# Retention, then a gated two-layer network, on one core: the first 64 positions loaded by pairs of heads in 2 KB runs

## The chip, the core and the metric

The kernel runs on one core of one Trainium2 chip. TensorE (PE) multiplies, VectorE (DVE), ScalarE (ACT) and GpSimd (POOL) work on tiles, SyncE (SP) and also ACT and POOL issue DMA transfers between HBM and the on-chip memories; TensorE writes to PSUM alone, and DVE and ACT bring its results from there to SBUF ("evict" below). The metric is the device time of one execution in microseconds (us), the median of several runs. A profile of one execution is shown beside it; times inside it count from the start of its span.

## What is computed

q, k and v are [8 batches, 8 heads, 576 positions, 64] in float32. Each head computes a decayed causal product, and the heads' outputs, side by side, go as 4608 tokens of 512 through a network with a hard swish:

```python
scores = scale * np.matmul(q, k.transpose(0, 1, 3, 2))
gamma = 1.0 - 2.0 ** (-5.0 - np.arange(H, dtype=np.float32))
Dmat = np.where(rel >= 0, gamma[:, None, None] ** rel[None, :, :], 0.0)
ret = scores * Dmat[None, :, :, :]
attn = np.matmul(ret, v)
x = attn.transpose(0, 2, 1, 3).reshape(B * S, H * D)
h = x @ w_in
g = h * np.clip(h + 3.0, 0.0, 6.0) / 6.0
out = g @ w_out
```

rel is the query's position less the key's; w_in is [512, 2048] and w_out [2048, 512].

## The kernel before

The tokens are worked in nine blocks of 512 (kb). Block 0 holds the first 64 positions (TL) of all eight batches; each later block is the other 512 positions of one batch, in four chunks of 128 with a running state per head. A block goes through the up projection (up_steps and up_pair: 16 units, each eight matmuls ph = win times xT for one 128-wide slice of d_ff, then u on ACT and the gated g on DVE) and the down projection (pd, or pm in a form with fewer products). TensorE's program interleaves the down projection of one block, the up projection of the next and the chunks of later ones. The order of all work is written out by hand: an engine runs its instructions in the order of the calls at the end of the kernel (L768 to L887), and a call that needs something late holds up what stands behind it on that engine.

The change lies in block 0, the head of the kernel. Its 64 x 8 = 512 tokens are four column groups c (NCB = 4) of 128: two batches, c and c + 4, of 64 positions each, since products of two batches are masked away. Its steps:

- load_half (L407) brings q and k in float32, one head for all batches at a time, with four positions (NJ = 4) of 64 numbers, 1 KB, side by side on a partition; a pair of neighbouring heads 2i and 2i + 1 fills a tile. The first k goes over SP and ACT, q over SP and ACT, the other keys over POOL, which also casts them to float16. The q of pairs 2 and 3 and the k of pairs 2 and 3 wait until the first half of k0 has landed (`behind`, `keys`).
- load_values (L422) brings v with one transfer from POOL into raw_v, the win pieces and then the wout pieces follow on the same queue. Loads of chunks 4 and up wait for the third wout piece (fetch, L838).
- indices and distances (L90, L113) make on POOL and DVE the position tables, a permutation by_chunk and the distances; mask_of_heads (L123) makes the decay masks of a pair on ACT.
- cast_heads (L435) casts q and the first k on DVE; turn_heads (L440) turns a tile with matmuls against by_chunk into PSUM (hpt, two banks, tag "st") and evicts it on ACT as kT or qT.
- scores_heads (L471) multiplies kT and qT (hpa) and masks the result on DVE (a16).
- values_heads (L463) orders the values of a pair with 16 matmuls (by_key, hpv) and evicts them on ACT into vh; inner_heads (L485) multiplies vh and a16 (hpo) and copies the result to xT of block 0.
- then the first four units of the up projection start, with the last inner product inside them (L823 to L831).
- during the up projection POOL and ACT make the decay tables (decays, L128) and POOL scales the keys, still by position on the partitions (others, L138); after it keys_heads (L466) orders them with 16 matmuls a pair (hpk) between the first products of the down projection, and head_states (L290) builds the states that the later blocks start from.

idle_products are matmuls whose result is not used; they keep TensorE active while it waits. PSUM has six banks of tag "pp" for hpa, hpv, hpo, hpk, ph and the idle products.

Of the kernel before, what the change touches and what calls it, by code (L numbers as in the profile page):

```python
# [21 lines left out]
def kernel(  # L22
# [13 lines left out]
    P = 128  # L36
# [30 lines left out]
    RP = TL // NJ  # L67
    ii = const.tile([P, NJ + 1], I32)
    ij = const.tile([P, NJ + 6], I32)
    fj = const.tile([P, NJ + 6], FP32)  # L70
    key, odd = fj[:, NJ + 3:NJ + 4], fj[:, NJ + 5:NJ + 6]
    arg = const.tile([P, NJ + 3, 2 * H], FP32)
    dec = const.tile([P, NJ + 3, 2 * H], FP32)
# [7 lines left out]
    dist, far = early[:, 0:P], early[:, P:2 * P]  # L81
    scale = const.tile([P, 1], FP32)
    FAR = 1.0e6
    by_chunk = const.tile([P, P], FP16)
    only = const.tile([P, 2], FP32)
    last = const.tile([P, 1], FP32)
    gpow = const.tile([P, NP], FP32)
    zh = [const.tile([P, NP, D], FP32, name=f"zh{b}") for b in range(B)]

    def indices():  # L90
        nc.vector.memset(half, 0.5)
        nc.gpsimd.iota(ii[:, 0:NJ], pattern=[[0, NJ]], base=0, channel_multiplier=1)
        nc.gpsimd.iota(ii[:, NJ:NJ + 1], pattern=[[1, 1]], base=0, channel_multiplier=1)
        nc.gpsimd.iota(query, pattern=[[TL, 2], [1, NJ], [NJ, RP]], base=0, channel_multiplier=0,
                       allow_small_or_imprecise_dtypes=True)
        make_identity(nc, ident16)
        p_ = ii[:, NJ:NJ + 1]
        nc.vector.tensor_scalar(ij[:, 0:NJ], ii[:, 0:NJ], P - B, 1, ALU.bitwise_and, ALU.logical_shift_right)
        nc.vector.tensor_copy(ij[:, NJ:NJ + 1], p_)
        for e in range(2):  # L100
            nc.vector.tensor_scalar(ij[:, NJ + 1 + e:NJ + 2 + e], p_, SUB - 1, 1, ALU.bitwise_and,
                                    ALU.logical_shift_left)
        nc.vector.tensor_scalar(ij[:, NJ + 3:NJ + 4], p_, RP - 1, 2, ALU.bitwise_and, ALU.logical_shift_left)
        nc.vector.tensor_scalar(ij[:, NJ + 4:NJ + 5], p_, 5, None, ALU.logical_shift_right)
        nc.vector.tensor_scalar(ij[:, NJ + 5:NJ + 6], p_, 4, 1, ALU.logical_shift_right, ALU.bitwise_and)
        nc.vector.tensor_copy(fj, ij)
        nc.vector.tensor_tensor(fj[:, 0:NJ], fj[:, 0:NJ], query[:, 0:TL:RP], ALU.add)
        nc.vector.tensor_scalar(fj[:, NJ:NJ + 2], fj[:, NJ:NJ + 2], 1.0, -float(P // 2), ALU.mult, ALU.add)
        nc.vector.tensor_scalar(fj[:, NJ + 2:NJ + 3], fj[:, NJ + 2:NJ + 3], 1.0, 1.0 - float(P // 2), ALU.mult, ALU.add)
        nc.vector.tensor_copy(by_chunk.rearrange("p (c e r) -> p c e r", c=NCB, e=2),  # L110
                              ident16.rearrange("p (r e c) -> p c e r", e=2, c=NCB))

    def distances():  # L113
        nc.vector.memset(scale, float(np.log(D ** -0.5)))
        nc.vector.tensor_tensor(key, key, fj[:, NJ + 4:NJ + 5], ALU.add)
# [5 lines left out]
        nc.vector.scalar_tensor_tensor(out=dist, in0=query, scalar=key, in1=far, op0=ALU.subtract, op1=ALU.add)  # L121

    def mask_of_heads(i):  # L123

        for h in (2 * i, 2 * i + 1):
            nc.scalar.activation(hmask[:, h, :], dist, ACTF.Exp, bias=scale, scale=float(np.log(gamma[h])))

    def decays():  # L128
        for h in range(H):
            lg = float(np.log(gamma[h]))  # L130
            nc.gpsimd.tensor_scalar(arg[:, :, h], fj[:, 0:NJ + 3], lg, float(np.log(D ** -0.5)),
                                    ALU.mult, ALU.add)
            nc.gpsimd.tensor_scalar(arg[:, :, H + h], fj[:, 0:NJ + 3], -lg, 0.0, ALU.mult, ALU.add)
# [784 lines left out]
```

## Time and profile before

| | us |
|---|---|
| median of 3 runs | 299.74 |
| lowest and highest | 299.30, 299.77 |
| the profiled execution | 299.44 |
| its span, first to last instruction | 297.7 |
| PE busy | 286.3 (96%) |
| DVE busy | 211.3 (71%) |
| ACT busy | 193.8 (65%) |
| POOL busy | 133.4 (45%) |

The mean granted clock of TensorE over the span is 0.994 of the full one. A row of the chain or of the timeline gives the start, the duration, the engine, the line of the kernel, the operation, what it writes and reads, and in brackets the idle time before it with what ended it. A row of the groups gives busy time, the mean of one instruction in ns, and the idle time before them. "PEld" is TensorE's loading of the stationary operand.

### The profile page before, as it was taken

Reading aid. Unit: us, or ns where it says so; the run is one execution under the profiler, and the core shown is the slowest. Engines: PE = TensorE matmul, PEld = TensorE weight load, DVE = VectorE, ACT = ScalarE, POOL = GpSimd, SP = SyncE. Lnnn points to the kernel's source line nnn. Section 1 sums busy time; section 2 is a strip of 40 time slices with the busy share of each in tenths; the row PEclk is TensorE's granted clock in tenths of the full one; section 3 lists DMA queues with packets and bytes.
Section 4 is the critical chain, followed back from the end, with each engine's and each line's share of the span. In section 5 each row is a group of like instructions: output and inputs, shape, how many; then the busy total and the mean of one; then the engine's idle time right before and its main releaser. Section 6 shows DMA issues by size and latency. Waiting matters only on the chain.

```text
span 297.7 us, 12581 instructions
## 1 busy us (share of the span) xinstructions
PE 286.3 (96%) x5552; PEld 218.8 (73%) x5552; DVE 211.3 (71%) x374; ACT 193.8 (65%) x350; POOL 133.4 (45%) x169
## 2 busy tenths in 40 slices
PE   5699999999999999999999999999999999999995
PEld 2467566788556667878988787787787788778894
DVE  5629636669885688798866887787769676647654
ACT  5659875789776687586758577566856665655420
POOL 7665078417851912539614862386256013100510
PEclk9979999999999999999999999999999999999999
DMA  7999998989999999998999999789907101200114
GB/s 163 188 205 216 217 233 206 213 184 221 135 214 221 203 205 196 167 234 191 228 244 194 184 216 174 144 168 263 144 27 118 74 2 39 104 5 2 73 73 141
DMA packets 119430, 47.86 MB, mean 161 GB/s; under 512 B 92240, under 2 KB 114768, under 8 KB 119376
## 3 DMA queue, kind: packets, MB, share of 16 engines
q1 hardware_dynamic: 114336, 41.56, 70.6%
q0 software_dynamic: 4608, 5.11, 10.4%
q8 instruction: 43, 0.70, 1.0%
q10 hardware_dynamic: 432, 0.39, 0.5%
q14 instruction: 11, 0.09, 0.2%
HBM read 36.70 MB, written 9.44 MB: 155 GB/s over the span
## 4 chain that ended last, share of the span: by engine, by line
PE 87%; DVE 4%; DMA 4%; ACT 3%; issue 1%; POOL 1%; ACTq 0%
PE ph L168 41%; PE pm L168 29%; PE pd L168 7%; PE po L250 4%; DMA raw_v<-in_v_dram 3%; PE pa L250 2%; DVE ws L552 2%; PE pu L250 1%; DMA hk<-in_k_dram 1%; ACT u L515 1%; DVE g L516 1%; DVE a L285 1%; POOL hk L416 1%; PE hpo L491 1%; PE hpv L459 1%
## 5 line engine op out<-in xcount | busy, mean ns | idle before, releaser
L168 PE MATMUL ph<-xT,win 128*64 128x512 f16 (+1 forms) x1248 | 144.9, 365 | 0.5 <-DVE g L516 0.3
L537 DVE SCALAR_TENSOR_TENSOR g<-u,ph 128x512 f16<-128x512 f32 x132 | 89.2, 683 | 48.5 <-ACT u L535 47.7
L535 ACT ACTIVATE u<-ph,half 128x512 f32<-128x512 f32 x132 | 90.2, 693 | 43.1 <-PE ph L168 40.6
L168 PEld LDWEIGHTS <-win 128*64 128x64 f16 x1248 | 84.5, 136 | 26.5 <-issue 1.9
L168 PEld LDWEIGHTS <-g 128*64 128x64 f16 x928 | 51.0, 110 | 15.6 <-issue 1.1
L168 PEld LDWEIGHTS <-s 128*64 128x64 f16 x896 | 49.9, 110 | 8.4 <-issue 0.5
L334 POOL TENSOR_TENSOR z<-z,gpow 128x256 f32<-128x256 f32 x24 | 16.4, 685 | 75.3 <-DVE z L333 46.9
L168 PE MATMUL pm<-ws,s 128*64 128x256 f16 x672 | 45.6, 273 | 0.1
L386 ACT CAST xT<-po 128x256 f16<-128x256 f32 (+1 forms) x44 | 22.5, 584 | 23.4 <-PE po L250 23.4
L211 POOL TENSOR_TENSOR q<-fq,dec 128x512 f16<-128x512 f32 x32 | 36.7, 1169 | 0.0
L214 POOL TENSOR_TENSOR v<-fv,dec 128x512 f16<-128x512 f32 x32 | 35.5, 1113 | 1.9 <-DMA fv<-in_v_dram 1.9
L168 PE MATMUL pd<-wout,g 128*64 128x512 f16 x256 | 35.0, 382 | 0.2 <-ACT o L581 0.2
L616 POOL TENSOR_TENSOR u<-u,p 128x512 f32<-128x512 f32 x7 | 8.9, 1271 | 54.0 <-ACT u L656 47.8
L168 PE MATMUL pm<-wout,g 128*64 128x256 f16 x448 | 31.6, 273 | 0.4 <-issue 0.4
L285 DVE TENSOR_TENSOR a<-pa,mask 128x256 f16<-128x256 f32 (+1 forms) x44 | 21.9, 539 | 7.8 <-PE pa L250 7.4
L203 ACT CAST k<-fk 128x512 f16<-128x512 f32 x32 | 19.8, 620 | 0.0
L552 DVE TENSOR_TENSOR s<-g 128x1024 f16<-128x1024 f16 x28 | 19.6, 702 | 0.2
L340 ACT CAST z<-z 128x512 f16<-128x512 f32 x24 | 15.0, 625 | 4.2 <-DVE z L330 3.9
L168 PE MATMUL pm<-ws,g 128*64 128x256 f16 x224 | 16.3, 273 | 0.0
L168 PE MATMUL pm<-wout,s 128*64 128x256 f16 x224 | 16.0, 273 | 0.1
L250 PE MATMUL po<-qT,z 64*64 64x64 f16 x512 | 12.6, 198 | 0.7 <-issue 0.4
L552 DVE TENSOR_TENSOR s<-g,s 128x1024 f16<-128x1024 f16 x14 | 12.6, 903 | 0.0
(112 smaller groups left out, 277.7 us busy)
## 6 DMA issues: line engine op xcount, KB each, us to landing
fq<-in_q_dram SPq DMA_DIRECT2D x16, 512.0 KB, 5.9
fk<-in_k_dram SPq DMA_DIRECT2D x32, 256.0 KB, 4.6
fv<-in_v_dram SPq DMA_DIRECT2D x32, 256.0 KB, 5.7
out_dram<-o SPq DMA_DIRECT2D x14, 512.0 KB, 3.2
wout<-in_moe_w_out_dram POOLq DMA_DIRECT2D x4, 512.0 KB, 18.5
out_dram<-o SPq DMA_DIRECT2D x7, 256.0 KB, 3.9
win<-in_moe_w_in_dram POOLq DMA_DIRECT2D x3, 512.0 KB, 13.4
hq<-in_q_dram SPq DMA_DIRECT2D x6, 128.0 KB, 5.0
```

Of the source, the lines that this page charges most:

```text
L168: nc.tensor.matmul(out[r], lhs[:, r], rhs, skip_group_check=True, **flags)
L203: keys = lambda: nc.scalar.copy(by_head(k16), in_rows(st[c]["fk"]))
L211: nc.gpsimd.tensor_tensor(by_head(q16[:, e]), in_rows(st[c]["fq"][:, :, e, :]), in_rows(dd[:, NJ + 1 + e, 0:H, :]), ALU.mult)
L214: nc.gpsimd.tensor_tensor(v16, st[c]["fv"], dd[:, NJ, H:2 * H, :], ALU.mult)
L250: return lambda: nc.tensor.matmul(*args, skip_group_check=True, **flags)
L285: nc.vector.tensor_tensor(a16[:, a, 0:n].rearrange("p x i q -> p (x i) q"), pa[a].rearrange("p x i q -> p (x i) q"), m, ALU.mult)
L334: nc.gpsimd.tensor_tensor(new, new, decay, ALU.mult)
L340: nc.scalar.copy(z16, zs[c])
L386: nc.scalar.copy(xt[:, s], po[s].rearrange("p x n (e r) -> p x n e r", e=2))
L535: nc.scalar.activation(uu, ph, ACTF.Relu, bias=half, scale=1.0 / 6.0)
L537: nc.vector.scalar_tensor_tensor(out=g[:, hf, :, jr, :], in0=by_half(uu), scalar=1.0, in1=by_half(ph), op0=ALU.min, op1=ALU.mult)
L552: nc.vector.tensor_tensor(*pend.popleft())
```

## The change

The pairs of heads become i and i + 4 (as in the rest of the kernel) in place of 2i and 2i + 1. A tile of q or k is loaded whole by one transfer, with eight positions (JL = 8) of a head, 2 KB, on a partition; the partition is (batch, which of the two heads, group of eight positions). No load waits for another. Turning a tile takes 16 matmuls against sel (64 columns for each of the two heads) in place of 8 against by_chunk; q is written back to the order of positions by the eviction, so the queries are in order and inner_heads copies straight.

The values are ordered by four heads at a time (g) and two column groups (y), eight matmuls of 256 columns each, and are evicted by ACT and DVE in turn, after all four scores. The inner products of column groups 0 and 2 of x come first, those of 1 and 3 follow inside the first units, whose order of the four slices becomes 0, 2, 1, 3; the two halves of the first win piece are slices 0 and 2, then 1 and 3. The fillers are 5, 2, 1, 1, 2 and a short 2 in place of 5, 4, 1, 1 and a short 5.

The keys for the states are now kT: POOL scales it by grown (four exponentials on ACT of a position table), and keys_heads turns it back with 8 matmuls against the identity in place of 16 with by_chunk. distances is folded into indices, which makes sel as well. The diff, cut to its core:

```diff
 def indices():
...
+        for e in range(2):
+            nc.vector.tensor_copy(sel[:, e], ident16.rearrange("p (y c e r) -> p e c y r", y=2, c=NCB, e=2)[:, e])
+        nc.vector.tensor_copy(by_chunk.rearrange("p (c y r) -> p c y r", c=NCB, r=RL),
+                              ident16.rearrange("p (r y c) -> p c y r", r=RL, c=NCB))
...
     def decays():
+        nc.gpsimd.iota(place, pattern=[[1, NJ], [NJ, 2], [0, 2], [JL, RL]], base=0, channel_multiplier=0,
+                       allow_small_or_imprecise_dtypes=True)
...
         nc.scalar.activation(dec, arg, ACTF.Exp)
+        for i in range(NP):
+            nc.scalar.activation(grown[:, i], place, ACTF.Exp, scale=rate[:, i:i + 1])
...
     def others():
         for i in range(NP):
-            k16 = hd[i]["k"].rearrange("p e j d -> p j e d")
-            dd = dec[:, 0:NJ, H + 2 * i:H + 2 * i + 2].unsqueeze(3).to_broadcast([P, NJ, 2, D])
-            nc.gpsimd.tensor_tensor(k16, k16, dd, ALU.mult)
+            kT = hd[i]["kT"]
+            nc.gpsimd.tensor_tensor(kT, kT, grown[:, i].unsqueeze(1).to_broadcast([P, NCB, P]), ALU.mult)
...
-    def load_half(i, nm, e, queue, behind=None):
...
+    def load_heads(i, nm, queue, behind=None):
...
+        d = queue.dma_start(t, dict(q=q, k=k)[nm][:, i::NP, 0:TL, :].rearrange("b e (r j) d -> (b e) r (j d)", j=JL))
...
     def turn_heads(i, nm, copy):
-        pt = psum.tile([P, NJ, P], FP32, tag="st", bufs=2, name=f"hpt{nm}{i}")
-        for j in range(NJ):
+        pt = psum.tile([P, JL, NCB, 2 * RL], FP32, tag="st", bufs=2, name=f"hpt{nm}{i}")
+        for j in range(JL):
+            at = j if nm == "q" else 2 * (j % NJ) + j // NJ
             for e in range(2):
-                nc.tensor.matmul(pt[e * D:e * D + D, j, :], hd[i][nm][:, e, j, :], by_chunk, start=True, stop=True,
+                nc.tensor.matmul(pt[e * D:e * D + D, at], hd[i][nm][:, j * D:j * D + D],
+                                 sel[:, e].rearrange("p c y r -> p c (y r)"), start=True, stop=True,
                                  skip_group_check=True)
...
+        if nm == "q":
+            t = half_tile(work, "qT", i, FP16, "hqT", bufs=3)
+            copy(t.rearrange("p (x j) -> p x j", j=JL), pt.rearrange("p j c y -> p (c y) j"))
+        else:
+            t = work.tile([P, H * D], FP16, tag="kT", bufs=4, name=f"hkT{i}")
+            copy(t.rearrange("p (c j y) -> p c j y", c=NCB, j=JL), pt.rearrange("p j c y -> p c j y"))
...
+    def values_heads(g, y, copy):
+        pv = psum.tile([P, 2, 2, 2, D], FP32, tag="pp", name=f"hpv{g}_{y}")
+        x = P // NJ
+        for c in range(2):
+            for j in range(NJ):
+                nc.tensor.matmul(pv[j * x:j * x + x, c], by_chunk[:, (2 * y + c) * x:(2 * y + c) * x + x],
+                                 raw_v[0][:, :, j, :].rearrange("p (e g h) d -> p g e h d", e=2, g=2)[:, g],
+                                 start=True, stop=True, skip_group_check=True)
+        copy(vh[:, 2 * y:2 * y + 2, g::2], pv)
+
+    def keys_heads(i):
+        kT = hd[i]["kT"]
+        pk = psum.tile([P, NCB, P], FP32, tag="pp", name=f"hpk{i}")
         for c in range(NCB):
...
+            product(pk[:, c], kT[:, c], ident16, start=True, stop=True)
...
+    def inner_heads(cc, copy):
...
+        copy(xts[0][:, cc, :], po.rearrange("p c x -> p (c x)"))
...
-        for dmc in range(NP):
+        for dmc in (0, 2, 1, 3):
...
-        win_piece(0, slice(NP // 2 * i, NP // 2 * (i + 1)))
+        win_piece(0, slice(i, NP, 2))
...
-        for nm in ("k", "q"):
-            landed = load_half(0, nm, 0, sp)
-            keys = landed if nm == "k" else keys
-            load_half(0, nm, 1, act)
+        load_heads(0, "k", sp)
+        load_heads(0, "q", act)
         nc.scalar.activation(warm, half, ACTF.Exp)
...
         for i in (1, 2, 3):
-            for e in range(2):
-                load_half(i, "k", e, pool, None if i == 1 else keys)
+            load_heads(i, "q", sp)
+            load_heads(i, "k", pool)
         load_values()
...
         idle_products(5)
         mask_of_heads(0)
+        mask_of_heads(1)
         cast_heads(0, "k", on_dve)
         turn_heads(0, "k", on_act)
-        mask_of_heads(1)
-        idle_products(4)
         cast_heads(0, "q", on_dve)
+        idle_products(2)
+        turn_heads(0, "q", on_act)
         mask_of_heads(2)
-        turn_heads(0, "q", on_act)
+        idle_products(1)
         turn_heads(1, "k", on_act)
...
         scores_heads(1)
+        turn_heads(3, "k", on_act)
+        turn_heads(3, "q", on_act)
+        scores_heads(2)
         idle_products(1)
-        turn_heads(3, "k", on_act)
-        scores_heads(2)
-        turn_heads(3, "q", on_act)
-        values_heads(0)
         scores_heads(3)
-        values_heads(1)
+        idle_products(2)
+        values_heads(0, 0, on_act)
+        values_heads(0, 1, on_dve)
+        values_heads(1, 0, on_act)
+        values_heads(1, 1, on_dve)
         inner_heads(0, on_act)
-        values_heads(2)
-        inner_heads(1, on_act)
-        values_heads(3)
         inner_heads(2, on_dve)
-        idle_products(5, 1)
+        idle_products(2, 1)
         first = [up_steps(0, u) for u in range(4)]
         for dmc in range(3):
             for unit in first:
                 next(unit)
-            if dmc == 1:
-                inner_heads(3, on_act)
+            if dmc == 0:
+                inner_heads(1, on_act)
+                inner_heads(3, on_dve)
```

More of the change, by code (lines that the diff above doesn't have):

```diff
@@ L80 @@
     early = io.tile([P, H, D], FP32, tag="fv", name="early").rearrange("p h d -> p (h d)")
-    dist, far = early[:, 0:P], early[:, P:2 * P]
+    dist, far, place = [early[:, P * n:P * n + P] for n in range(3)]
+    grown = io.tile([P, H, D], FP32, tag="fv", name="grown").rearrange("p h d -> p (h d)").rearrange("p (i x) -> p i x", i=NP)
     scale = const.tile([P, 1], FP32)
     FAR = 1.0e6
+    sel = const.tile([P, 2, NCB, 2, RL], FP16)
     by_chunk = const.tile([P, P], FP16)
@@ L87 @@
     gpow = const.tile([P, NP], FP32)
+    rate = const.tile([P, NP], FP32)
     zh = [const.tile([P, NP, D], FP32, name=f"zh{b}") for b in range(B)]
@@ L110, in indices @@
[L110 to L115, printed above, removed]
+        nc.vector.tensor_scalar(ij[:, 0:1], pidx, RL - 1, 3, ALU.bitwise_and, ALU.logical_shift_left)
+        nc.vector.tensor_scalar(ij[:, 1:2], pidx, 2, 4, ALU.logical_shift_right, ALU.bitwise_and)
@@ L420, in load_half @@
         return d
+    raw_v = []
     def load_values():
```

136 lines of the change are left out of this document (53 added, 83 removed).

## The prediction, made before the changed kernel was run

> **What bounds the kernel now.** I read the page first, for the engine that sets the span.
>
> ```profile
> span 297.7 us, 12581 instructions
> PE 286.3 (96%) x5552; PEld 218.8 (73%) x5552; DVE 211.3 (71%) x374; ACT 193.8 (65%) x350; POOL 133.4 (45%) x169
> ```
>
> PE is busy 96% of the span, so once its dense work runs, whatever brings that work forward ends the kernel as much earlier. The change touches only the head, so the next view is the chain that ended last, in order of time, over the first 45 us (start, duration, what).
>
> ```profile
> 0.82 3.06 DMA hk<-in_k_dram
> 3.88 0.28 issue
> 4.16 2.00 POOL hk L416 x4
> 6.17 7.92 DMA raw_v<-in_v_dram
> ...
> 14.12 0.41 PE hpv L459 x16
> ...
> 15.21 0.41 PE hpo L491 x8
> ...
> 18.23 2.27 PE ph L168 x8
> 20.50 0.22 PE hpo L491 x4
> 20.72 12.13 PE ph L168 x110
> 32.85 0.34 PE hpk L459 x16
> ...
> 43.18 0.22 PE ptk L168 x8
> ```
>
> The reader is to see one chain: k0 lands at 3.88, that lets POOL issue four held key loads, behind them it issues the value load, and only its landing at 14.08 starts the values, the inner products and, at 18.2, the up projection (ph). From there PE is dense. Third, the windows between the edges of the granted clock (columns: stretch, its length, busy us of each engine with its instructions, PEclk, DMA share, GB/s written).
>
> ```profile
> 5.55:8.96 3.41, 1.87 (x38) 1.14 (x34) 1.50 (x2) 2.50 (x8) 3.41 (x6) 1.00 1.18 234
> 12.37:15.79 3.42, 1.65 (x64) 1.17 (x63) 2.37 (x5) 1.38 (x4) 0.72 (x2) 1.00 1.21 180
> 15.79:19.20 3.41, 3.41 (x63) 2.24 (x50) 1.15 (x2) 2.00 (x5) 3.02 (x16) 0.50 1.24 205
> ```
>
> After a stretch with PE busy 1.65 of 3.42 us (48%) the clock is at half from 15.79 to 19.20; after one with 1.87 of 3.41 (55%) it stayed full. The half clock covers the inner products and the first 1.2 us of ph.
>
> **Part by part: the loads.** The eight q loads of 128 KB become four of 256 KB and the eight k loads four; runs grow from 1 to 2 KB; nothing waits for k0 any more. Windows by what the DMA moves (same columns):
>
> ```profile
> 2.28:3.20 0.92, 0.92 (x6) 0.35 (x4) 0.89 (x8) 0.92 (x1) 0.89 (x2) 1.00 0.84 267
> 3.20:5.20 2.00, 1.84 (x16) 0.79 (x14) 1.12 (x5) 1.21 (x5) 1.04 (x3) 1.00 0.99 196
> 10.40:12.00 1.60, 1.54 (x26) 0.80 (x24) 1.25 (x3) 1.19 (x3) 1.41 (x3) 1.00 1.38 181
> 20.00:25.00 5.00, 5.00 (x56) 3.81 (x54) 2.40 (x4) 3.71 (x8) 1.00 (x4) 1.00 1.21 213
> ```
>
> The hold leaves the queues short: 196 GB/s where 267 had just been moved, over 2.0 us, which is (267-196)/267 x 2.0 = 0.5 us lost. For the run length the trace has raw_v alone at 10.4 to 12 (1 KB read, 512 B written: 181 GB/s) and win alone at 20 to 25 (2 KB read, 1 KB written: 213): doubled runs move 18% more. The time of q and k before is 14.08 - 2.28 less raw_v's own 0.524 MB / 181 GB/s = 2.9 us, so 8.9 us; at 18% more it saves 1.4 us. raw_v then lands at 14.08 - 0.5 - 1.4 = 12.2. Bounds: 14.08 (nothing won, since the bytes are the same and the DMA is already full) and 11.6 (q and k at 267 GB/s: q 1.05 MB, k0 0.26 and the cast keys 0.39 are 1.70 MB written, 6.4 us, then 2.9). I take 12.2, nearest to the two rows with one load alone. Against the longer runs speaks the Trainium skill, DMA: Bandwidth & Descriptors, section Specifications, which puts the line rate at 512 B a transfer and above; by it only the 0.5 us of the hold is won, raw_v lands at 13.6, the up projection starts some 0.4 us later than forecast below and the time is 296.7. The trace's 181 against 213 GB/s disagrees.
>
> POOL's queue: it issues three key loads in place of six, with no wait, ahead of raw_v, the win and wout pieces.
>
> ```profile
> 1.84 1.33 POOL L416 DMA_DIRECT2D hk<-in_k_dram  x2
> ...
> 7.04 3.70 POOL L681 DMA_DIRECT2D win<-in_moe_w_in_dram  x5
> ```
>
> At 1.33/2 = 0.67 each raw_v is issued at 3.85 instead of 6.17, and win at 4.7 instead of 7.04. SP issues four loads in place of seven, ACT one in place of three. k0 (now whole, on SP) shares the DMA with q0: at worst 256 KB more ahead of it at 267 GB/s, 1.0 us; I take 0.4, so k0 lands at 4.3, when DVE is also through with its index work (three small copies for sel and by_chunk, and the distances now ahead of the cast). q0 lands with it; before, its eviction began at 7.78 (below).
>
> **The chain of turns.** With raw_v early, what is late next is ACT: it evicts all eight turned tiles and makes the masks.
>
> ```profile
> 4.05 0.69 ACT L126 ACTIVATE ws<-early,scale 128x128 f16<-128x128 f32 x2 [0.39 <-DVE early L121]
> ...
> 5.61 1.27 ACT L126 ACTIVATE ws<-early,scale 128x128 f16<-128x128 f32 x4
> 7.78 0.58 ACT L450 CAST hqT<-hptq 128x512 f16<-128x512 f32 x1 [0.89 <-PE hptq L444]
> 8.26 0.59 ACT L450 CAST hkT<-hptk 128x512 f16<-128x512 f32 x1
> 8.87 0.58 ACT L450 CAST hqT<-hptq 128x512 f16<-128x512 f32 x1
> 9.35 0.69 ACT L126 ACTIVATE ws<-early,scale 128x128 f16<-128x128 f32 x2
> ...
> 12.04 0.58 ACT L450 CAST hqT<-hptq 128x512 f16<-128x512 f32 x1 [0.21 <-PE hptq L444]
> ```
>
> Masks 0.69 + 1.27 + 0.69 = 2.65 us, eight evictions at a step of 0.55 (7.78 to 8.87 holds two) = 4.4. From 4.05 without a wait that ends at 11.1; with 0.3 for the first tiles I take 11.4, where it now ends at 12.62. The turn is 16 matmuls of 64 columns in place of 8 of 128; the nearest row is pu below, 16 of that shape in 0.25 us against 0.22, so PE (1.87 of 3.41 us busy) hides it.
>
> ```profile
> 38.57 0.25 PE pu L296 x16
> ```
>
> ```profile
> L482 DVE TENSOR_TENSOR ha<-hpa,ws 128x512 f16<-128x512 f32 x8 | 5.0, 676 | 1.1 <-PE hpa L478 1.1
> L493 ACT CAST xT<-hpo 128x512 f16<-128x512 f32 x3 | 1.8, 598 | 3.0 <-PE hpo L491 3.0
> L493 DVE CAST xT<-hpo 128x512 f16<-128x512 f32 x1 | 0.7, 692 | 1.5 <-PE hpo L491 1.5
> ```
>
> The eviction of q now reads PSUM in steps of 64 floats. Bounds: nothing (L493 already reads in steps of 16 floats and takes 598 ns, as an eviction in order does), or a multiple of 0.58 us (rival below); I take nothing. All four scores now stand ahead of the values, so DVE's eight products come first: the pair of scores(2) starts near 11.1, that of scores(3) ends at 11.1 + 4 x 0.65 = 13.7 (bounds 13.1, when the pair of scores(3) waits only for its own PE work at 11.8, and 14.2). After it come DVE's half of the first four value heads, 0.69 (14.4), the inner product, 0.41 (14.8), and ACT's copy, 0.60: **ph starts at 15.4** and not 18.02. raw_v at 12.2 lies beside DVE's products; with it at 14.08 ph starts at 16.4 (0.34 values, again 0.34, then 0.69 + 0.41 + 0.60 and a step of 0.1 between).
>
> **The up projection.** Its first two dmc need inner 0 and 2 and the first half of win; two inner products instead of one now stand inside it: +0.22 (the row at 20.50).
>
> ```profile
> 18.02 2.48 PE L168 MATMUL ph<-xT,win 128*64 128x512 f16 x16
> 20.34 0.39 PE L491 MATMUL hpo<-ha,ws 128*64 128x128 f16 x8
> 20.56 12.29 PE L168 MATMUL ph<-xT,win 128*64 128x512 f16 x112
> ```
>
> At 12.29/112 = 0.110 us the first 16 would take 1.76 and not 2.32: the half clock costs ph 0.56. In the new order PE's wait between the values and the first inner product is near 0.7 us, and from 12.37 to 15.79 I count 2.4 us of PE work (values 1.3, inner 0.8, fillers and ph 0.3), 70%, so I forecast no half clock: -0.56. By the Trainium skill, TensorE: Matmul & The Clock Gate, Part 1, the clock falls only after a whole idle window of about 3.4 us; by it a stretch with 1.65 us of work could not have halved the clock, the -0.56 would want another cause, and rival B would have no chance. The trace shows half clock behind just that stretch, so B keeps one.
>
> Weights: the third win piece, first needed by unit 4, lands 11.6 us (the median of five) after its issue at about 8.5, at 20.1. With the DMA 1.9 earlier that is 18.2; unit 4 starts at 15.4 + 16 x 2 x 0.110 + 0.44 = 19.4. Hidden, and still hidden (by 0.3) with the hold's 0.5 alone.
>
> ```profile
> DMA to landing us min/median/max: 8.3/11.6/15.2
> ```
>
> ACT gains four exponentials (grown, 1.27 us together by the mask row) behind the fourth ph unit.
>
> ```profile
> L535 ACT ACTIVATE u<-ph,half 128x512 f32<-128x512 f32 x132 | 90.2, 693 | 43.1 <-PE ph L168 40.6
> ```
>
> Four units end together and leave ACT 4 x 0.69 = 2.8 us of work, 0.7 of it done as the last one ends; with 0.3 for dec (about one mask), 1.27 for grown and unit 4's own 0.69 on ACT and 0.69 on DVE its bank is free 5.1 us after that end. PE comes back to the bank six units later, 6 x 8 x 0.110 = 5.3 us. Hidden by a hair; uncovered it could cost no more than the 1.27. POOL's others() is again four passes of 128x512, 1.04 each by the POOL row further down, beside the 14 us of ph.
>
> **keys_heads** becomes 8 matmuls in place of 16 at a place where PE is the chain: 0.34 (the row at 32.85) against 0.22 (at 43.18, the same shape): 4 x 0.12 = -0.48.
>
> The loads of chunk 4, released by a wout landing, need not come as much earlier as PE does:
>
> ```profile
> 33.97 1.33 SPq L189 DMA_DIRECT2D fv<-in_v_dram  x1
> ```
>
> ```profile
> 41.94 1.04 POOL L214 TENSOR_TENSOR v<-fv,dec 128x512 f16<-128x512 f32 x1
> ```
>
> With the page's median of 5.7 fv lands at 39.7, 2.2 before its use; 3.4 earlier against 1.9 leaves 0.7. Hidden.
>
> **Sum.** -2.62 (15.4 for 18.02) + 0.22 - 0.56 - 0.48 = -3.44. The profiled execution took 299.44 (span 297.7 and 1.74 around it), so 296.0; the median of the runs, 299.74, stands 0.30 above it, and I forecast **296.3**.
>
> **Rivals.**
> B: the clock still falls, and its 3.41 us at half lie wholly inside ph: +1.7, 298.0. For it: the 48% row; against it: my count of 70%. What decides is whether a stretch ends under about half busy.
> C: the loads come no sooner, as the same bytes go through a DMA that is already over 1.0 in share: ph at 16.4, 297.3. Against it: 196 beside 267 GB/s.
> D, slower: the eviction of q by steps of 64 floats. It stands four times on ACT's path, which has no slack left. It decides from 3.44/4 = 0.86 us more each (1.44 in place of 0.58); at three times 0.58 it costs 4.6, so 300.9. For it: no row reads so wide a step with runs of one; against it: 598 ns at 16.
> N: the change does not do what it says, q and k arrive as late as before, and ACT ends at 12.6 as now; only keys_heads gains: 299.3.
>
> **How the numbers follow.** The likeliest case has 0.48 (its own range 294.6 to 297.3: if DVE's products are done when raw_v lands at 11.6, ph starts at 14.0, 294.9, less 0.3 for the spread of the runs; raw_v at 13.6 gives 296.7 and k0 late by the full 1.0 another 0.6), B 0.18, C 0.08, N 0.06, D 0.20 (three to four times 0.58: 300.9 to 303.2). 0.2% is 0.6 us, about what a measurement can tell from no change: faster 0.74, same 0.06, slower 0.20. The range 294.6 to 300.4 takes in the forecast's own, B, C and N and leaves out D.
>
> **What would show it.** No wait of POOL between its key loads, raw_v landing near 12.2, L450's counterpart for q still at 0.58 us, ACT without waits from 5 to 11.4, ph starting near 15.4 with PEclk 1.0 beside it, keys at 0.22. The forecast is wrong if q's evictions show over 0.8 us, if the row of windows shows 0.50 after 15, or if ph, once started, waits for win.

## The result and the profile after

| | before, us | after, us | ratio, 95% interval |
|---|---|---|---|
| first comparison, medians of 10 and 10 runs | 299.80 | 297.77 | 0.9939 [0.9916, 0.9962] |
| the changed kernel once more, medians of 17 and 12 | 299.03 | 297.96 | 0.9953 [0.9927, 0.9979] |

The change makes the kernel faster by 0.5 to 0.6%, 1.1 to 2.0 us; 3.4 were forecast. Its profiled execution took 297.56. The page of the changed kernel, first two lines:

```profile
span 295.9 us, 12570 instructions
PE 284.7 (96%) x5546; PEld 221.7 (75%) x5546; DVE 212.4 (72%) x376; ACT 192.7 (65%) x351; POOL 134.0 (45%) x177
```

The span is 1.8 us shorter and PE busy 1.6 less: as before, PE is busy 96% of it. The chain of waits of the changed kernel (start, duration, what), to set beside the one of before:

```profile
0.82 4.68 DMA hk<-in_k_dram
...
5.52 0.56 DVE hk L442
...
6.12 0.64 PE hptk L450 x16
6.76 0.85 PE idle L174 x4
7.62 0.44 PE hptq L450 x16
...
8.08 0.59 ACT hqT L455
...
13.91 1.27 DVE ha L489 x2
15.18 0.61 DVE ws L469
...
15.83 0.32 PE hpo L498 x4
...
16.81 1.08 PE ph L174 x8
...
31.92 4.74 ACT ws L477 x8
...
36.70 0.22 PE pu L302 x2
...
41.28 0.22 PE ptk L174 x8
```

raw_v is gone from the chain. What stands in its place is k0: the first keys land at 5.50, not at 3.88, and from there DVE's cast, the turns on PE, ACT's evictions and masks and DVE's products follow one another until ph starts at 16.81. Further down, ACT's eight scaled copies of the turned keys, 4.74 us in a row, hold PE at pu. The timeline of the changed kernel (start, duration, engine, line, operation, and in brackets the wait before it) answers the steps one at a time:

```profile
1.72 1.82 POOL L421 DMA_DIRECT2D hk<-in_k_dram  x3
...
3.49 0.89 POOL L431 DMA_DIRECT2D raw_v<-in_v_dram  x1
...
6.80 0.59 ACT L458 CAST hkT<-hptk 128x512 f16<-128x512 f32 x1 [1.71 <-PE hptk L450]
8.08 0.59 ACT L455 CAST hqT<-hptq 128x512 f16<-128x512 f32 x1 [0.69 <-PE hptq L450]
...
9.78 0.44 PE L450 MATMUL hptk<-sel,hk 128*64 128x64 f16 x16
...
9.79 1.29 DVE L489 TENSOR_TENSOR ha<-hpa,ws 128x512 f16<-128x512 f32 x2
...
11.32 3.85 DVE L489 TENSOR_TENSOR ha<-hpa,ws 128x512 f16<-128x512 f32 x6
...
12.30 0.59 ACT L455 CAST hqT<-hptq 128x512 f16<-128x512 f32 x1
...
13.02 0.53 POOL L694 DMA_DIRECT2D wout<-in_moe_w_out_dram  x1 [2.13 <-DMA raw_v<-in_v_dram]
```

POOL's queue went as forecast, without a wait; the wout load that waits for raw_v starts at 13.02. In the traces whose chain shows the landing of raw_v this load starts 0.28 or 0.29 behind it, so raw_v lands at 12.73 here (the expectations below say 12.69). The forecast had ACT run without waits: it waits 1.71 us for the first turn of k and 0.69 for the first of q, and its eighth eviction ends at 12.89 (12.30 + 0.59), not at 11.4. DVE's first products start at 9.79, and from there its eight products, with one cast of q between them, run without a wait to 15.18. The eviction of q takes 0.59 and a turn 0.44 at the full clock, 0.64 at half. The clock: windows between its edges (columns as in the prediction), first of the changed kernel, then of a second profile of the kernel before.

```profile
5.80:9.21 3.41, 3.09 (x70) 2.36 (x70) 1.26 (x3) 1.72 (x5) 2.82 (x5) 1.00 1.15 260
9.21:12.62 3.41, 2.93 (x95) 2.31 (x91) 3.25 (x6) 3.37 (x9) 0.66 (x2) 1.00 1.41 206
12.62:16.03 3.41, 2.75 (x58) 1.55 (x60) 3.33 (x6) 1.34 (x3) 1.64 (x5) 1.00 1.23 202
```

```profile
11.47:14.88 3.41, 2.60 (x78) 1.85 (x74) 3.11 (x7) 2.44 (x5) 0.87 (x2) 1.00 1.28 178
...
```

A reader must know here that the record of the clock begins with the first full stretch, at 9.21 and 11.47 in these two; rows before it show 1.00 though the turns still take 0.64 us. In the two stretches behind it the changed kernel has PE busy 2.93 and 2.75 of 3.41 us (81% and more), and the clock stays full. The second profile of before had no late half clock either, unlike the first.

The marks of seven traces, in us: the landing of k0, that of raw_v, the first ph, the key turn of chunk 4 (ptk, where the head of the kernel ends), the time between these two, and the span.

| kernel | k0 | raw_v | first ph | ptk | between | span |
|---|---|---|---|---|---|---|
| before | 3.88 | 14.08 | 18.02 | 42.99 | 24.97 | 297.7 |
| before, second profile | 3.87 | 13.92 | 17.23 | 42.05 | 24.82 | 296.4 |
| after | 5.50 | 12.73 | 16.81 | 41.09 | 24.28 | 295.9 |
| after, second profile | 5.36 | 13.31 | 16.82 | 41.10 | 24.28 | 295.6 |
| before without the hold | 3.9 | 13.26 | 16.57 | 40.95 | 24.38 | 295.6 |
| the same, second profile | 3.9 | 13.64 | 16.95 | 41.33 | 24.38 | 296.6 |
| after with k0 on ACT | 4.46 at the latest | 12.54 | 15.80 | 40.07 | 24.27 | 294.5 |

From the first profile of before to that of after the key turn comes 1.90 earlier: 1.21 at the start of ph, 0.59 where ph ran at half clock (24.97 against the 24.38 of a trace of the old order at full clock) and 0.10 elsewhere. Behind the key turn the seven executions take 254.4 to 255.3 us, so a difference of less than 1 us between two spans cannot be put down to the head.

### The profile page after: what moved, and what is told of

Same layout as the page of the kernel before. It is cut to its first block, busy times and chain, and to the rows that moved or that the text cites. A ratio compares the mean times of both kernels' runs of the same rounds, so it can differ in the third digit from the quotient of the medians.

```text
span 295.9 us, 12570 instructions
## 1 busy us (share of the span) xinstructions
PE 284.7 (96%) x5546; PEld 221.7 (75%) x5546; DVE 212.4 (72%) x376; ACT 192.7 (65%) x351; POOL 134.0 (45%) x177
## 3 DMA queue, kind: packets, MB, share of 16 engines
HBM read 36.70 MB, written 9.44 MB: 156 GB/s over the span
## 4 chain that ended last, share of the span: by engine, by line
PE 86%; ACT 6%; DVE 5%; DMA 2%; issue 1%; ACTq 0%
PE ph L174 41%; PE pm L174 29%; PE pd L174 6%; PE po L256 4%; PE pa L256 2%; ACT ws L477 2%; DVE ws L559 2%; DMA hk<-in_k_dram 2%; PE pu L256 1%; ACT u L522 1%; DVE g L523 1%; DVE a L291 1%; PE idle L174 1%; PE ptq L174 1%; ACT hqT L455 1%
## 5 line engine op out<-in xcount | busy, mean ns | idle before, releaser
L174 PEld LDWEIGHTS <-win 128*64 128x64 f16 x1248 | 85.7, 136 | 24.7 <-issue 1.4
L174 PEld LDWEIGHTS <-g 128*64 128x64 f16 x928 | 51.6, 110 | 15.0 <-issue 1.2
L340 POOL TENSOR_TENSOR z<-z,gpow 128x256 f32<-128x256 f32 x24 | 16.4, 685 | 72.9 <-DVE z L339 46.9
L256 PEld LDWEIGHTS <-z 64*64 64x64 f16 x512 | 8.1, 105 | 6.3 <-issue 1.7
```

The lines of the kernel that those rows point to most:

```text
L174: nc.tensor.matmul(out[r], lhs[:, r], rhs, skip_group_check=True, **flags)
L256: return lambda: nc.tensor.matmul(*args, skip_group_check=True, **flags)
L340: nc.gpsimd.tensor_tensor(new, new, decay, ALU.mult)
```

## The experiments

**What the executions' clocks say.** Each timed run lists the mean granted clock of its execution. One half stretch of 3.41 us in a span of 297 lowers it by 0.0057. The 77 executions of the kernel before that were timed beside the experiments, on several chips, fall into three groups, and the 22 of the changed kernel (10 and 12) into one:

| | mean clock | executions | mean time, us |
|---|---|---|---|
| before | 0.998 and over, no half stretch | 28 | 298.66 |
| before | 0.992 to 0.994, one | 37 | 299.70 |
| before | 0.989, two | 12 | 300.74 |
| before, all | | 77 | 299.48 |
| after | 0.998 and over | 22 | 297.98 |

Executions with one half stretch took 1.04 us longer in the mean than those without, executions with two 2.08. The profiles agree with the size: from raw_v's landing to the first ph the first profile of before takes 3.94 us, the second and both without the hold 3.31, which is 0.63, and inside ph it is 0.59, so 1.22 together. On the mean the change gains 1.50 us: at 1.04 a stretch 0.82 because none of its executions has one ((37 x 1.04 + 12 x 2.08) / 77), and 0.68 against the executions of before that had none either. The executions come from several chips, so this split is an estimate.

**The keys on the other queue.** In the changed kernel k0 (on SP) and q0 (on ACT) are issued at the same instant, and k0 lands second.

```diff
-        load_heads(0, "k", sp)
-        load_heads(0, "q", act)
+        load_heads(0, "k", act)
+        load_heads(0, "q", sp)
```

> The changed kernel, with the first keys (k0) loaded over ACT and the first q over SP, instead of the other way round. Theory 1: k0 is late (it landed at 5.50, before the change at 3.88) because the transfer issued on SP gets its first packets through behind the whole 256 KB of the one on ACT; then k0 lands near 4.4 (where q0 landed), q0 near 5.5, the first turn starts near 5.0 instead of 6.12, and the up projection (ph) starts 0.5 to 0.9 earlier than 16.81; the time falls by that, to 297.0. Theory 2: k0 is late because nothing is held any more and q1 and the other keys share the DMA with it; then k0 lands no earlier than 5.2 and the time stays at 297.8.

Median 297.41 (12 runs), ratio 0.9927 [0.9900, 0.9954]. In its timeline the cast and the first turn of k0:

```profile
4.46 0.43 DVE L442 CAST hk<-hk 128x512 f16<-128x512 f32 x1
...
4.94 0.64 PE L450 MATMUL hptk<-sel,hk 128*64 128x64 f16 x16 [0.78 <-DVE hk L442]
```

The cast starts 1.06 earlier than the 5.52 of after, ACT's eighth eviction ends 1.18 earlier (11.71) and ph starts 1.01 earlier, with the first full clock at nearly the same time (9.35 against 9.21): in this profile k0's lateness went straight through to ph. The DMA queues show the order: from 2.28 to 3.20 us only ACT's queue moves packets in the trace of after (73), where in before ACT's and SP's move 144 and 117 side by side; with k0 and q0 exchanged it is ACT's again (78 packets to 1), so what ACT issues goes first, whichever load it is. The 1.01 us is one profile's: in the two others with this exchange, below, ph starts at 16.52 and 17.48. The mean of the time over 12 runs is 297.40 against 297.98 over the 22 of after; the two ratios' intervals overlap.

**DVE between its products and the inner products.** values_heads(0, 1) is evicted on DVE, which is busy with products until 15.17; the first inner product waits for it.

```diff
-        values_heads(0, 1, on_dve)
-        values_heads(1, 0, on_act)
+        values_heads(0, 1, on_act)
+        values_heads(1, 0, on_dve)
```

> The changed kernel, with both evictions of the values of column groups 0 and 2 on ACT and both of 1 and 3 on DVE. Theory 1: ph waits for DVE, whose eight masked products end at 15.17 and whose eviction of half the values comes behind them (15.79); with that eviction on ACT, idle there, the first inner product starts near 15.4 and ph near 16.3 instead of 16.81, 297.3. Theory 2: ph waits for TensorE's own order or for the landing of raw_v or win; then ph starts at 16.8 as it does now, 297.8.

Median 297.28 (8 runs), ratio 0.9926 [0.9893, 0.9959]. The chain of waits of this kernel:

```profile
14.27 1.08 ACT ws L469 x2
...
15.40 0.32 PE hpo L498 x4
...
16.38 1.08 PE ph L174 x8
```

DVE is off the chain, the inner product starts 0.43 earlier and so does ph. The 0.43 us is a mark of the trace; the times alone do not resolve it.

**The fillers of the changed kernel.** Eight before the first turn, and none between the turns.

```diff
-        idle_products(5)
+        idle_products(8)
...
-        idle_products(2)
         turn_heads(0, "q", on_act)
         mask_of_heads(2)
-        idle_products(1)
```

> The changed kernel, with the fillers moved: 8 before the first turn in place of 5, and none between the first turns in place of 2 and 1. Theory 1: the fillers between the turns stand on the path (0.85 us at half clock between k0's and q0's turn), and the idle stretch ahead of k0 keeps the clock at half until 9.2; then q0's eviction starts near 7.2 instead of 8.08, the clock is full by about 6, and ph starts 0.3 to 0.8 earlier, 297.2. Theory 2: ACT's own chain and the landings of q1 and k2 set the pace whatever TensorE does early; then ph starts within 0.2 of 16.8, 297.8.

Median 297.52 (12 runs), ratio 0.9948 [0.9919, 0.9977]. Its profile came out the other way; the windows between its clock edges:

```profile
4.79:8.20 3.41, 1.50 (x52) 0.99 (x48) 0.81 (x2) 1.90 (x6) 2.75 (x5) 1.00 1.06 244
8.20:11.61 3.41, 2.59 (x72) 2.13 (x64) 2.24 (x4) 2.46 (x7) 1.73 (x3) 0.50 1.34 220
11.61:15.03 3.42, 3.42 (x60) 1.94 (x54) 3.17 (x7) 1.46 (x3) 0.53 (x1) 0.50 1.26 205
```

The clock rose earlier, then found a stretch with PE busy 44% and fell for two, and ph started at 17.66. Of its 12 executions 7 had a full clock, 3 one and 2 two half stretches; after had none in 22. So where the fillers stand decides how often the clock falls, though the median is no worse than that of after. The rows show too that a busy share of 76% (2.59 of 3.41) did not bring a half clock back up; the full stretch behind it did.

**Fillers into the kernel before.** Eight ahead of its wait for raw_v, to measure the half clock by itself.

```diff
         turn_heads(3, "q", on_act)
+        idle_products(8)
         values_heads(0)
```

> The kernel before, with 8 fillers where TensorE waits for raw_v (12.0 to 14.1). Theory 1: the half clock from 15.79 to 19.20 came of that wait, and costs the inner products and the first 16 ph some 1.0 and 0.56; then PEclk stays at 1.00 there, ph starts near 17.0 instead of 18.02, and the time falls by 1.5 to 298.3 (ratio 0.995), most of what the whole change won. Theory 2: the clock falls for another reason; then the windows show 0.50 again and the time stays at 299.8.

Median 301.30 (12 runs), ratio 1.0056 [1.0027, 1.0085]: slower. All 12 had a full clock, and first ph to ptk took 24.42, as it should; but ph started at 17.92 and not at 17.0, 3.77 us behind the landing of raw_v (14.15), and the rest of the span grew from 254.7 to 256.8. The chain of waits of this kernel from 120 to 145 us has steps that wait for nothing the profile shows, each 0.5 to 0.6 long:

```profile
125.46 0.54 issue
...
128.34 0.50 issue
...
140.06 0.60 issue
```

The chain of after has none there. What makes them is open; the second profile of before has one such gap of PE's weight loads (0.53 us) inside its first ph products, which is 0.44 of its 24.82. The experiment shows that the half clock costs about 0.6 inside ph (24.42 against 24.97), not what the fillers would be worth; and since 12 executions with a full clock are slower here than before, a full clock alone does not bring the 1.04 us.

**Swap, eviction and a split of the key copies.** The two edits that gained, and every second of the copies L477 on DVE.

```diff
-            nc.scalar.mul(kn[e][:, i], pk, only[:, e:e + 1])
+            if e == 0:
+                nc.scalar.mul(kn[e][:, i], pk, only[:, e:e + 1])
+            else:
+                nc.vector.tensor_scalar(kn[e][:, i], pk, only[:, e:e + 1], None, ALU.mult)
```

> The changed kernel with three edits together: k0 over ACT and q0 over SP; the values of column groups 0 and 2 evicted on ACT and those of 1 and 3 on DVE; and of the two scaled copies of each turned key pair (the rows L477) one on ACT and one on DVE. Theory: the three remove three different waits of the path, k0's landing (1.01 us by its own run), DVE's queue ahead of the first inner product (0.43) and ACT's eight scaled copies, 4.74 us in a row ahead of the first state product (up to 0.35); ph starts near 15.4 and the first state product stands 16.9 us behind its start in the place of 18.1 to 18.9 before, the time is near 296.4. Rival: the edits overlap, because with k0 early DVE or raw_v becomes the bound, and the time is that of the swap alone, 297.4.

Median 297.15 (9 runs), ratio 0.9934 [0.9904, 0.9965]: the rival's side. The chain of waits of this kernel where the copies stand:

```profile
33.41 0.68 DVE ws L480 x2
34.09 0.60 issue
34.70 0.45 DVE ws L562
...
36.64 0.67 DVE ws L480
...
37.35 0.22 PE pu L302 x2
```

DVE alternates the copies with its weight sums (L562), and one step of 0.60 waits for nothing that the profile shows, so the last copy ends no earlier: from the first ph to the pu that waits for it, 37.35 - 17.48 = 19.87, against 36.70 - 16.81 = 19.89 (the first pu of all starts 19.04 behind ph in both, not 16.9). Its head of the chain was not repeated from the kernel with the swap alone: here the keys of pair 1 landed at 8.22, the clock came up only at 14.58, and ph started at 17.48.

**The length of the runs.** The changed kernel with every q and k load cut in two of 1 KB runs; the bytes and their places stay.

```diff
-        d = queue.dma_start(t, dict(q=q, k=k)[nm][:, i::NP, 0:TL, :].rearrange("b e (r j) d -> (b e) r (j d)", j=JL))
+        src = dict(q=q, k=k)[nm][:, i::NP, 0:TL, :].rearrange("b e (r j) d -> (b e) r (j d)", j=JL)
+        for x in range(2):
+            y = slice(JL * D // 2 * x, JL * D // 2 * (x + 1))
+            d = queue.dma_start(t[:, y], src[:, :, y])
```

> The changed kernel with each load of q and k split into two transfers of half the row, 1 KB a run in place of 2 KB (as before the change), twice as many transfers, nothing else. Theory 1: a run of 2 KB moves 15 to 18% more per us, so with 1 KB raw_v lands 1.0 to 1.4 later than 12.69, near 13.9. Theory 2: the packets of 1 KB and 2 KB move nearly the same (in the traces 320 packets of 1 KB a us before, 172 of 2 KB after, 328 and 352 KB), and raw_v came earlier because POOL issues it at 3.49 instead of 6.17; then raw_v lands within 0.6 of 12.69.

A single time, 297.71. Windows by what the DMA moves (last column GB/s), of the changed kernel and then of this one:

```profile
3.20:5.20 2.00, 0.97 (x6) 0.09 (x2) 1.19 (x5) 1.28 (x4) 2.00 (x4) 1.00 1.07 283
5.20:8.20 3.00, 2.08 (x38) 1.41 (x40) 1.30 (x3) 0.71 (x2) 2.99 (x4) 1.00 1.13 253
```

```profile
3.20:5.20 2.00, 0.97 (x6) 0.09 (x2) 0.90 (x5) 1.72 (x6) 2.00 (x5) 1.00 0.92 155
5.20:8.20 3.00, 1.05 (x20) 0.80 (x22) 1.33 (x3) 0.37 (x1) 3.00 (x5) 1.00 1.24 253
```

From 5.20 to 8.20 us, 1 KB runs and 2 KB runs both move 253 GB/s (the second profile of after 227), so there the length of the runs makes no difference that stands out of the scatter. What the whole tiles win is before that, 283 against 155, less what they lose in the 0.92 us ahead of it (from 2.28 to 3.20 they move 163, the halves 274): some 0.15 MB by 5.20. Why is open. The edit changes the length of the runs and the number of transfers together; an engine needs as long to issue 128 KB as 256 (six key loads held POOL from 1.72 to 5.10, three from 1.72 to 3.54), but with the DMA's share at 0.92 it is not shown that it lacked issued loads. k0 landed at 6.58. raw_v landed at 13.32, between the two theories and inside the 12.5 to 13.9 of the changed order's other profiles, so it decides nothing. ph started at 17.88, 1.07 later than in after, and still the span is 296.0 against 295.9: behind the key turn this execution took 253.9 us, 0.9 less than after.

**The hold alone.** The kernel before, with no load waiting for k0.

```diff
-                load_half(i, "q", e, sp, keys)
+                load_half(i, "q", e, sp)
...
-                load_half(i, "k", e, pool, None if i == 1 else keys)
+                load_half(i, "k", e, pool)
```

> The kernel before, with no load waiting for k0's landing any more, nothing else. Theory 1: the hold costs the DMA some 0.5 us of empty queues and raw_v its place; raw_v is issued near 5.3 instead of 6.17 and lands near 13.4 instead of 14.08, ph starts 0.3 to 0.7 earlier than 18.02, with k0 still near 3.9 because it has both hardware queues first. Theory 2: the hold only reorders a DMA that is full anyway; raw_v lands at 14.0 as it did and ph starts at 18.0.

A single time, 297.26. The chain of waits of this kernel:

```profile
2.63 2.53 POOL hk L416 x5
5.17 8.09 DMA raw_v<-in_v_dram
```

Its window where the prediction had seen the queues short (last column GB/s):

```profile
3.20:5.20 2.00, 1.77 (x16) 0.79 (x14) 1.20 (x5) 1.14 (x4) 2.00 (x5) 1.00 0.93 184
```

raw_v is issued 1.00 earlier than in before and lands 0.82 earlier, k0 is no later (3.9), and ph starts at 16.57. The DMA moves no more without the hold: 184 GB/s here and 153 in the second profile, where the two profiles of before have 196 and 160. It moves more only later, from 8.20 to 10.40: 246 and 235 against 205 and 217. So what the hold cost is raw_v's place in POOL's queue, and not the supply between 3.20 and 5.20. A single time does not price half a per cent; timed several times:

> The kernel before with no load held, as in the single look, now timed. Theory (the hold is what the change is worth, the other parts net nothing): 297.6 to 298.0, ratio to before 0.993 to 0.995, no different from the changed kernel. Rival (the single look was a lucky run, and the hold alone is worth only its 0.5 us of queue supply): 299.0 or more.

Median 298.33 (9 runs), ratio 0.9950 [0.9926, 0.9975]: the interval leaves out 1, so there is a gain, and takes in both ratios of the change. Of the 10 executions, the single one among them, 8 had a full clock, their mean 297.82; the two with one half stretch 298.72 and 299.06.

**The hold put back.** The changed kernel with the loads of pairs 2 and 3 waiting for k0.

```diff
-        load_heads(0, "k", sp)
+        keys = load_heads(0, "k", sp)
...
-            load_heads(i, "q", sp)
-            load_heads(i, "k", pool)
+            load_heads(i, "q", sp, None if i == 1 else keys)
+            load_heads(i, "k", pool, None if i == 1 else keys)
```

> The changed kernel with the q and k of pairs 2 and 3 held until k0 has landed, as before the change. Theory 1: k0 lands at 5.5 as it does without the hold, because it is q0's transfer on ACT that goes ahead of it; POOL then issues raw_v near 7.2 and it lands near 14.9, and ph starts near 18.0. Theory 2: the loads of pairs 2 and 3 crowd k0; with the hold it lands at 4.6 or sooner.

A single time, 299.05. The chain of waits and the windows of this kernel:

```profile
0.82 4.57 DMA hk<-in_k_dram
...
6.79 8.59 DMA raw_v<-in_v_dram
...
18.29 1.47 PE ph L174 x8
```

```profile
12.35:15.76 3.41, 1.71 (x30) 0.89 (x30) 2.84 (x5) 0.38 (x1) 0.18 (x2) 1.00 1.30 197
15.76:19.18 3.42, 3.38 (x54) 2.30 (x44) 2.08 (x3) 1.76 (x3) 2.67 (x12) 0.50 1.24 206
```

k0 is as late (5.39) with nothing but q0 and pair 1 beside it, so it is not the crowd of later loads that delays it. From 3.20 to 5.20 us the DMA moves 272 GB/s with the hold, about as much as without (283). And the picture of before is back whole: raw_v on the chain, PE waiting, a stretch 50% busy, a half clock, ph at 18.29.

**Swap and eviction together.**

> The changed kernel with both edits that gained alone: k0 issued by ACT and q0 by SP, and the eviction of values_heads(0, 1) on ACT, of values_heads(1, 0) on DVE. Theory 1 (the two gains lie one behind the other on one path: k0's lateness ahead of the turns, DVE's queue between its products and the first inner product): the gains add to 1.0 + 0.4 us, ph starts at 15.4, chunk 4's key turn at 39.7, span 294.2, time 296.4. Rival (they cover the same wait: with the swap the products on DVE end earlier, ACT is the later engine and takes the eviction no sooner than DVE would): ph at 15.8 as with the swap alone, span 294.5, time 297.1 or more.

Median 297.88 (7 runs), ratio 0.9941 [0.9920, 0.9961]: no better than the change. Its chain of waits:

```profile
3.49 10.43 DMA raw_v<-in_v_dram
...
13.96 0.43 PE hpv L466 x8
...
16.52 1.08 PE ph L174 x8
```

With the turns and DVE earlier, raw_v is late again, and in this execution it took 10.43 us and not the 9.2 of after. ph starts 0.14 later than with the eviction alone (16.38). Two of the 7 executions had a half stretch. The gains do not add, but not for the rival's reason: ACT was not the later engine, the landing of raw_v was. No version here is shown to beat the change.

**Both kernels once more**, to learn how far the marks scatter.

> The changed kernel once more, unaltered, to learn how far its marks scatter between two profiles. Theory (the scatter of raw_v's landing is the 0.4 us seen between the two profiles of the kernel before without a hold, 13.26 and 13.65, and the up projection's start does not hang on it): k0 cast at 5.5 +-0.1, raw_v landing 12.3 to 13.1, ph at 16.8 +-0.2, half clock only up to 9.2, span 295.9 +-0.4, time 297.8, ratio 0.993 to 0.995. Rival (raw_v's landing scatters by more than 1 us whatever the edit, 12.5 with the swap and 13.9 with swap and evictions): raw_v at 13.7 or later, and ph later with it.

> The kernel before once more, unaltered. Theory (its late half clock is a property of its order of work): clock half for one stretch again between 15 and 20, ph at 18.0 +-0.3, first ph to chunk 4's key turn 24.9 to 25.0, span 297.7 +-0.4. Rival (the half clock hangs on where the stretches happen to fall): clock full behind 9, first ph to the key turn 24.4, ph at 17.7 or earlier, span 296.8 or less.

The chain of the changed kernel repeats to 0.02 at ph (16.82 and 16.81), though raw_v landed 0.58 later, at 13.31 and just outside what was expected: up to there ph does not hang on it, while at 13.91, with k0 and the eviction early, it did. raw_v lay between 12.5 and 13.9 in the seven profiles of the changed order with whole tiles and no hold. The kernel before does not repeat: in its second profile the clock came up only at 11.47, so the early turns ran slower, PE waited 0.81 for raw_v in place of 2.12, the stretch was 76% busy (2.60 of 3.41) and nothing fell. So the half clock is no fixed property of its order, as that theory had it, but an outcome in 49 of 77 executions.

## Why the prediction was right in sign and half right in size

**Bound, POOL's queue, the values off the path: right.** The loads bound the head, POOL issues raw_v at 3.49 (3.85 forecast), it lands at 12.73 and 13.31 (12.2 forecast, up to 14.08 allowed), beside DVE's products.

**The start of ph: the mis-sized term.** -2.62 was forecast, -1.21 measured. The forecast end of the path was right: from the end of DVE's products to ph 1.63 (15.18 to 16.81), forecast 1.7. The products end at 15.18 and not at 13.7. DVE runs them without a wait from 9.79, so what is late is their first, which needs the first turned tiles; ACT's evictions are late by as much (12.89 and not 11.4). The step that failed is "From 4.05 without a wait that ends at 11.1; with 0.3 for the first tiles I take 11.4": the 0.3 for the first tiles measured 2.40 us, ACT's waits of 1.71 and 0.69, and the same lateness is in the scores that DVE starts from. Behind the first wait stands "I take 0.4, so k0 lands at 4.3": k0 lands at 5.50, beyond the bound of 1.0 as well, because the sum had k0 share the DMA with q0, while it comes second to it. The swap shows the price in one profile: 1.06 earlier at the cast, 1.01 at ph. The second wait, 0.69, is the same with the swap. There the turns take 0.64 at half clock, which lasted to 9.21 in place of 5.55, with four fillers (0.85) between them on the chain, where the prediction had PE hide the turns; no run isolates it.

**The run length: wrong.** "Doubled runs move 18% more" read two different loads, values and weights, as a difference of run length. From 5.20 to 8.20 us the two lengths move 253 GB/s each. That they differ by 18% is not seen. The Trainium skill, DMA: Bandwidth & Descriptors, section Specifications, which asks for 512 B for line rate, agrees with these rows, against my reading of the trace. That raw_v still came 0.6 to 1.4 earlier goes with its earlier issue (3.49 against 6.17) and the whole tiles' 0.15 MB; no run parts the two.

**The hold: right that it costs, wrong where.** It was given 0.5 us of DMA supply, from 196 GB/s beside 267. Without it the same two microseconds move 184 and 153, so the loss is not where the prediction read it. Dropping it alone in the kernel before gives a ratio of 0.9950 where the whole change gives 0.9939 and 0.9953. What it wins is raw_v's earlier place in POOL's queue, and with it a shorter wait, in which the clock falls less often (2 of 10 executions against 49 of 77). That the rest of the change nets nothing is what the intervals allow, not what they prove; in it k0's lateness and the better head stand against each other.

**The clock: right in sign and in the profile.** 0.56 was forecast for the half clock in ph, and 0.59 is what the first profile of before lost. As a mean over executions the half clock is worth some 0.82 by the groups, of which a part lies ahead of ph. Rival B is refuted in 22 of 22 executions of the changed kernel; that its 298.0 is the nearest to 297.77 of all the times given is luck. The busy shares behind which the clock fell, 44, 48 and 50% (a_fill, before, a_hold), are not whole idle windows, so the rule of the Trainium skill, TensorE: Matmul & The Clock Gate, Part 1, as I had weighed it, does not hold here as stated; what the same part says of the window, that it runs free of the kernel's start, fits the two profiles of before, with first edges at 5.55 and 11.47.

**Up projection and keys: won, and mostly lost again.** The extra inner product (+0.22) and the keys (-0.48) were to net -0.26; 24.28 against the 24.38 without the hold is -0.10. From the first ph to the first turned keys it is 14.26 against 14.17 us, +0.09. From there to the first pu it is 4.78 against 5.62, -0.84, more than forecast, because the down products between the turns come quicker as well. But from the first pu to the next down product it is 0.90 against 0.25, +0.65: ACT's copies L477, 0.59 each and back to back, now end the wait. The prediction looked at PE's row and not at who is next.

**Grown, weights, chunk 4: hidden**, as forecast; ph never waits for win in the trace, and the four exponentials show no idle PE behind them.

**The other rivals.** D is refuted by one row: the eviction of q takes 0.59. C is right that the longer runs move no more, but raw_v came earlier all the same and is not what starts ph (its terms add up to 16.6 and not to 16.4). N's time is refuted, and raw_v and the last q and k landed earlier; one of its marks came true for another reason, for ACT ends at 12.89, as late as before (12.62).

## What to carry to other kernels

When a wait disappears, price first what is late next, and look at the very first transfers: one loaded whole and issued at the same instant as another may come second to it, and in a head without slack that microsecond can go through to the work behind it. A hold that keeps loads back for an urgent one also moves whatever is issued behind them on the same queue, and its worth should be measured by dropping it alone. If a kernel's executions fall into groups by granted clock, compare the groups' counts and their means, since one profile shows only one of the outcomes.

## What the runs showed of the hardware

- Two 256 KB loads issued at 0.82 on SP and ACT landed one behind the other, not together: k0 on SP at 5.36 to 5.50 in four profiles, at 4.46 or before with the two exchanged. From 2.28 to 3.20 ACT's queue moved 73 packets and SP's none, with the two exchanged 78 and 1.
- In the heads, with the clock full, it fell behind stretches of 3.41 us with PE 44, 48 and 50% busy and stayed full behind 55% (1.87 of 3.41) and more. The share alone does not decide: at the end of the second profile of before it stayed full behind 1.63 of 3.41 us (48%). A half clock came back up behind 80% (2.74 of 3.41, in the second profile of after) and not behind 76% (2.59).
- The same program had its first full clock at 5.55 in one execution and at 11.47 in another, and the later one ended earlier: its slower early turns left PE 0.81 us of wait for raw_v in place of 2.12, and the clock did not fall.
- Runs of 1 KB and 2 KB both moved 253 GB/s from 5.20 to 8.20 us. Just ahead of it, from 3.20 to 5.20, the kernels with loads of 128 KB moved 153 to 196 GB/s and those with loads of 256 KB 262 to 300, with and without a hold. Which of run length and number of transfers makes that is open.
- Stalls of 0.5 to 0.8 us in which an engine waits for nothing that the profile shows come in some executions and not in others; eight more fillers at the head went with three of them after 125 us. Their cause stays open.
